# A prologue that loads x three quarters by crossbar and one quarter through TensorE

## The chip, the cores and the metric

One core of a Trainium2 chip. The metric is device microseconds (us) of one execution. A profile gives the span of one execution (about 1.8 us less than the time) and the mean clock that TensorE was granted, 1.0 being full. All runs told here were correct. The batches of runs (e1 to e4, e5 to e8, e9 to e12) carry different chip numbers in the record, so times are compared within a batch, or as ratios to the kernel before in the same rounds.

## The reference

Two branches share one input x (2048 x 640, bf16): a gated long convolution, and an attention with 32 query heads over one key/value head of width 20. A sigmoid gate mixes them.

```
g = sigmoid((x * gate_w).sum(-1))
q = x @ wq   (32 heads of 20);  k = x @ wk;  v = x @ wv
b = softmax(q k^T / sqrt(20)) v, heads joined, @ wo
a = x * (conv(kv, ssm_k) + kv * ssm_D),  kv = shift_conv(k_in) * v_in
out = g * a + (1 - g) * b
```

## The kernel before

The program is planned statically. Python code adds operations with planned costs and dependencies to a graph; a list scheduler places each on an engine at a planned time; each engine then gets its instructions in that order and waits on semaphores. An engine takes the next instruction of its list and nothing else (in the changed kernel q's first projection had its operands at 10.27 us and started at 13.34, behind a block that TensorE was still waiting for), so a wrong planned time becomes a wrong order.

```python
# Scheduler.place: the plan's model of a DMA
begin = max(start + 0.1, self.dma_bw)
self.dma_bw = begin + op.nbytes / 300e3
op.end = self.dma_bw + op.lat          # lat is 2.2 unless given
self.t[e] = start + 0.35
# pick_pe: dummy matmuls on TensorE where its planned load is low (FILL = 0.5)
if (... self.main_started and self.can_fill and m is not None and gap > 0.1
        and self.busy_in(t, 2.4) < FILL):
    f = Op("pe", self.filler, ...)
...
# loads: x transposed by the DMA crossbar, in four blocks of 512 tokens
for b in range(NB):
    o = T["xT"][:, :, 512 * b:512 * b + 512]
    i = aps["A_q"][0][512 * b:512 * b + 512, :]
    xl = self.g.add("sp", lambda e, o=o, i=i: e.dma_start_transpose(o, i), (), [("xT", b)], 0.1,
                    kind="d", nbytes=1000000, prio=-8 + b)
...
# kproj: kT groups, then k/v/gate projections per block ("kvn"), their squares, max over all blocks
gr = self.group("kT", (1.16 if b == 0 else 4.0) + 0.1 * b, banks=ALLB)
...
# qproj: needs xT block 0 and the padded wq; squares -> q2 -> "ci"; with the max of k: a row of
# bounds "cr", sent by DMA into qT ("crow"); the first scores (QK) need that row
```

So before the first score, ScalarE's first exponential can't start: k of all four blocks, its maximum, the row, its DMA. After that the kernel is 970 exponentials of 128x1024 on ScalarE, with everything else placed around them.

Of the kernel before, what the change touches and what calls it, by code (L numbers as in the profile page):

```python
# [21 lines left out]
class Op:  # L22
    __slots__ = ("eng", "fn", "deps", "cost", "kind", "name", "prio", "grp", "alts", "port", "nbytes", "main",
                 "cont", "nun", "succ", "ready", "start", "end", "placed", "sig", "value", "lane", "known", "seq",
                 "banks", "last", "floating", "tail", "attached", "lat")

    def __init__(self, eng, fn, cost, kind, name, prio):
        self.eng = eng
        self.fn = fn
        self.deps = set()  # L30
        self.cost = cost
        self.kind = kind
        self.name = name
        self.prio = prio
        self.grp = None
        self.alts = None
        self.port = False
        self.nbytes = 0
        self.main = False
        self.cont = False  # L40
        self.nun = 0
        self.succ = []
        self.ready = 0.0
        self.start = None
        self.end = None
        self.placed = False
        self.sig = False
        self.value = None
        self.lane = None
        self.known = None  # L50
        self.seq = -1
        self.banks = None
        self.last = False
        self.floating = False
        self.tail = ()
        self.attached = False
        self.lat = 2.2


class Group:  # L60
# [74 lines left out]
class Scheduler:  # L135
# [177 lines left out]
    def place(self, op, e):  # L313
        t = self.t[e]
        op.eng = e
        if op.alts:
            for x in op.alts:
                self.cand[x].discard(op)
            op.fn, op.cost = op.alts[e]
        else:  # L320
            self.cand[e].discard(op)
        if op.main and e == "pe":
            for b in op.banks or ():
                if not self.bank_claimed[b]:
                    self.bank_claimed[b] = True
                    op.deps.update(self.bank_last[b])
        start = max(t, op.ready)
        if op.kind == "d":
            begin = max(start + 0.1, self.dma_bw)
            self.dma_bw = begin + op.nbytes / 300e3  # L330
            op.end = self.dma_bw + op.lat
            self.t[e] = start + 0.35
            best = min(range(NLANES), key=lambda l: self.lanes[l][-1].end if self.lanes[l] else -1.0)
            op.lane = best
            if self.lanes[best]:
                op.deps.add(self.lanes[best][-1])
            self.lanes[best].append(op)
            op.value = 16 * len(self.lanes[best])
        else:
            if (op.port and e == "dve") or e == "pool":  # L340
                start2 = max(start, self.port_until)
                op.end = start2 + op.cost
                self.port_until = op.end
            else:
                op.end = start + op.cost
            self.t[e] = op.end
        op.start = start
        op.placed = True
        if e == "pe" and op.cost > 0.05:
            self.active.append((op.end - op.cost * 0.92, op.end))  # L350
        if op.name == "pv":
            self.can_fill = not op.last
        self.order[e].append(op)
        self.linear.append(op)
        gr = op.grp
        if gr is not None:
            if e == "pe" and op in gr.mms:
                gr.pos += 1
                if gr.pos == len(gr.mms):
                    self.open = None  # L360
            elif op in gr.evacs:
                if all(x.placed for x in gr.evacs):
                    b = gr.bank
                    self.bank_busy[b] = False
                    self.bank_last[b] = [gr.mms[-1]] + list(gr.evacs)
                    self.bank_ready[b] = max(x.end for x in gr.evacs) + LAT
        for s in op.succ:
            s.nun -= 1
            lat = 0.0 if (s.eng == "pe" and e == "pe") else LAT
            s.ready = max(s.ready, op.end + lat)  # L370
            sg = s.grp
            if sg is not None and s.eng == "pe" and not (op.grp is sg):
                sg.nun -= 1
                sg.ready = max(sg.ready, op.end + lat)
                if sg.nun == 0:
                    self.gcand.add(sg)
            if s.nun == 0:
                self.enable(s)
# [72 lines left out]
NSC, NDC, NB = 16, 5, 4  # L451
# [37 lines left out]
class Kernel:  # L489
# [163 lines left out]
    def loads(self):  # L653
        T, aps = self.T, self.aps
        x = aps["A_q"][0].rearrange("(i p) d -> p i d", p=128)
        self.dma(T["wkv"][:, :, 0:20], aps["B_wk"].rearrange("(dc p) c -> p dc c", p=128), writes=["wk"],
                 nbytes=50000, eng="act", prio=-98.8)
        self.dma(T["wkv"][:, :, 20:40], aps["B_wv"].rearrange("(dc p) c -> p dc c", p=128), writes=["wv"],
                 nbytes=50000, eng="act", prio=-98.7)
        wq = aps["B_wq"].rearrange("(dc p) n -> p dc n", p=128)  # L660
        self.dma(T["gw5"][:, :], aps["gate_w"].rearrange("(dc p) -> dc p", p=128), writes=["gw5"], nbytes=2000,
                 eng="act", prio=-98.5)
        self.dma(T["wqst"][:, :, 0:160], wq[:, :, 0:160], writes=[("wqst", 0)], nbytes=204800, eng="act", prio=-98.9)
        xl = None
        for b in range(NB):
            o = T["xT"][:, :, 512 * b:512 * b + 512]
            i = aps["A_q"][0][512 * b:512 * b + 512, :]
            xl = self.g.add("sp", lambda e, o=o, i=i: e.dma_start_transpose(o, i), (), [("xT", b)], 0.1, kind="d",
                            nbytes=1000000, prio=-8 + b)

        self.xl = [xl]
        self.dma(T["wqst"][:, :, 160:640], wq[:, :, 160:640], writes=[("wqst", 1)], nbytes=614400, prio=-4,
                 after=self.xl)
        self.dma(T["Dbc"][:, :], aps["A_ssm_D"].partition_broadcast(128), writes=["Dbc"], nbytes=163840, prio=30,
                 after=self.xl)

    def consts(self):
# [16 lines left out]
        P(lambda e: e.memset(T["vaug"][:, :, 20:21], 1.0), (), ["vaug"], 0.3, prio=-8)  # L694
        identv = T["ident"][:, :].rearrange("p (r c) -> p r c", c=32)
        V(lambda e: e.tensor_reduce(T["acol"][:, :], identv[:, :, 0:20], AX.X, ALU.add), ["ident"], ["acol"], 0.3,
          prio=-4)
        V(lambda e: e.tensor_reduce(T["mcol"][:, :], identv[:, :, 20], AX.X, ALU.add), ["ident"], ["mcol"], 0.2,
          prio=-5)
        V(lambda e: e.tensor_scalar(T["mcol"][:, :], T["mcol"][:, :], -1.0, None, ALU.mult), ["mcol"], ["mcol"], 0.2,  # L700
          prio=-5)
        V(lambda e: e.tensor_reduce(T["altcol"][:, :], T["ident"][:, 1:128:2], AX.X, ALU.add), ["ident"], ["altcol"],
          0.3, prio=-3)
        V(lambda e: e.tensor_scalar(T["altcol"][:, :], T["altcol"][:, :], -2.0, 1.0, ALU.mult, ALU.add), ["altcol"],
          ["altcol"], 0.2, prio=-3)
        for n, ng in (("IndG2", 2), ("IndG4", 4)):
            P(lambda e, n=n: e.memset(T[n][:, :, :], 0.0), (), [n], 0.2, prio=-7)
            for gl in range(ng):
                V(lambda e, n=n, gl=gl, ng=ng: e.tensor_copy(T[n][:, gl, gl:4 * ng:ng], T["acol"][:, :]), ["acol"],
                  [n], 0.2, prio=-2 if ng == 2 else 20)  # L710

        V(lambda e: e.memset(T["scl0"][:, :], 2.0 / L), (), ["scl0"], 0.1, prio=12)
        V(lambda e: e.memset(T["scl0"][0:1, :], 1.0 / L), (), ["scl0"], 0.1, prio=12)
# [77 lines left out]
    def weights2(self):  # L791
# [5 lines left out]
        for q in range(1, 4):  # L797
            self.pool(lambda e, q=q: e.tensor_copy(dst[:, :, 8 * q:8 * q + 8, 0:20], src[:, :, 8 * q:8 * q + 8, :]),
                      [("wqst", 1)], [("wq_pad", 1)], 1.5, prio=-4, name="wq_cp")

    def load_x(self):
        T = self.T
        x = self.aps["A_q"][0].rearrange("(i p) d -> p i d", p=128)
        for b in range(NB):
            self.dma(T["xn"][:, 4 * b:4 * b + 4, :], x[:, 4 * b:4 * b + 4, :], writes=[("xn", b)], nbytes=655360,
                     prio=30 + b, name="ld_x", after=self.crow0)

    def kproj(self):
# [3 lines left out]
        gr = self.group("gwt", 0.0, banks=ALLB)  # L812
        self.mm(gr, lambda e, bk: e.transpose(self.bank_bf(bk, NDC), T["gw5"][:, :], T["ident"][0:NDC, 0:NDC]),
                ["gw5", "ident"], 0.1)
        self.evac(gr, "dve", lambda e, bk: e.tensor_copy(T["wkv"][:, :, 40], self.bank_bf(bk, NDC)), (), ["wg"], 0.2)
        for b in range(NB):
            gr = self.group("kT", (1.16 if b == 0 else 4.0) + 0.1 * b, banks=ALLB)
            self.kTg.append(gr)
            for dc in range(NDC):
                self.mm(gr, lambda e, bk, b=b, dc=dc: e.matmul(  # L820
# [47 lines left out]
    def qproj(self, I, gs, prio, banks, ng):  # L868
# [22 lines left out]
        for gl in range(ng):  # L891
# [9 lines left out]
        self.dve(lambda e: e.tensor_scalar(cr[0:n, :], ci[0:n, :].bitcast(F32), T["kmaxr"][0:n, 0:1], -UP,  # L901
                                           ALU.mult, ALU.add), ["ci", "kmaxr"], ["cr"], c_fast(512), prio=pr, name="root")
        o = self.dma(qt[20:128:32, gs[0]:gs[0] + ng, :], cr[0:n, :], reads=["cr"],
                 writes=[("qT", par, gi) for gi in gs], nbytes=n * 1024, prio=pr, name="crow")
        if I == 0 and gs[0] == 0:
            self.crow0 = [o]

# [443 lines left out]
    def build(self):  # L1351
# [2 lines left out]
        self.consts()  # L1354
        self.tables()
        self.weights()
        self.kproj()
        ALLB = (7, 5, 4, 3, 2, 1, 0)
        for b in range(4):
# [81 lines left out]
```

## Time and profile before

| part of the profiled execution | us |
|---|---|
| up to the first exponential | 24.3 |
| stream of exponentials, first start to last end | 893.5 |
| of which ScalarE waits (stream less its busy time) | 2.9 |
| tail | 9.2 |
| span | 927.0 |
| time, median of the three runs at hand | 928.67 (927.61 to 930.36) |

The three parts add up to the span, so a change of the prologue is read from the first line. The prediction shows the lines of the profile.

### The profile page before, as it was taken

To read this page: it belongs to the slowest core of one execution; us is meant where nothing else is said; L and a number is where in the kernel's file an instruction comes from. 1 tells how busy PE (TensorE), PEld (TensorE's weight loads), DVE (VectorE), ACT (ScalarE), POOL (GpSimd) and SP (SyncE) were. 2 spreads that over 40 slices of the span, in tenths; PEclk is the share of its full clock that TensorE was granted. 3 is DMA by queue.
4 is the path that set the end of the run, shared out by engine and by line. 5 is a ranking of instruction groups with operands and counts; after the bars stand their busy time and mean duration, and the time that the engine had idled before them with its cause. 6 is when DMAs were issued, how large, how long until landed. Compare 5 with 4: busy or idle time off the path is not lost.

```text
span 927.0 us, 16240 instructions
## 1 busy us (share of the span) xinstructions
PE 802.8 (87%) x6829; PEld 332.5 (36%) x6829; DVE 607.5 (66%) x810; ACT 901.0 (97%) x989; POOL 377.9 (41%) x331
## 2 busy tenths in 40 slices
PE   8777788889999889999898899988999889888786
PEld 3222113433344334444343344443444433332232
DVE  6667883566675665676776677567667665567564
ACT  4999999999999999999999999999999999999996
POOL 2960001768714227733267333488433882000000
PEclk9999989999999999999999999999999997999999
DMA  7822532001000001000001020000000003111100
GB/s 159 288 74 89 195 121 65 13 9 39 19 19 19 19 8 35 19 19 19 18 14 30 19 54 18 19 13 8 18 19 18 13 13 82 38 55 49 34 13 28
DMA packets 42998, 41.83 MB, mean 45 GB/s; under 512 B 22739, under 2 KB 36173, under 8 KB 42925
## 3 DMA queue, kind: packets, MB, share of 16 engines
q1 hardware_dynamic: 40659, 40.22, 14.3%
q8 instruction: 53, 0.87, 0.4%
q10 hardware_dynamic: 2266, 0.59, 0.3%
q14 instruction: 20, 0.16, 0.1%
HBM read 31.76 MB, written 6.02 MB: 41 GB/s over the span
## 4 chain that ended last, share of the span: by engine, by line
ACT 93%; PE 5%; DVE 0%; issue 0%; DVEq 0%; POOL 0%; POOLq 0%
ACT ET L950 93%; PE ps L1386 1%; PE ps L934 1%; PE ps L1382 1%; PE ps L976 1%; PE ps L820 0%; PE ps L1232 0%; PE ps L1094 0%; PE ps L876 0%; PE ps L1296 0%; PE ps L1178 0%; DVE outsb L1116 0%; PE ps L1101 0%; PE ps L834 0%; DVEq L445 0%
## 5 line engine op out<-in xcount | busy, mean ns | idle before, releaser
L950 ACT ACTIVATE ET<-ps 128x1024 bf16<-128x1024 f32 x970 | 890.6, 1198 | 5.7 <-PE ps L934 5.1
L934 PE MATMUL ps<-qT,kT 21*128 21x512 bf16 x2048 | 225.0, 389 | 107.3 <-ACT ET L950 101.0
L1263 POOL TENSOR_TENSOR Pp<-X,K 128x512 f32<-128x512 bf16 x120 | 163.3, 1387 | 286.7 <-DVE K L1251 286.7
L976 PE MATMUL ps<-ET,vaug 128*32 128x512 bf16 x1940 | 208.8, 394 | 1.0 <-ACT ET L950 1.0
L934 PEld LDWEIGHTS ps<-qT,kT 21*128 21x128 bf16 x2048 | 56.4, 91 | 275.3 <-ACT ET L950 267.3
L964 DVE TENSOR_SCALAR dJ<-ps 128x1024 uint32<-128x1024 f32 x54 | 66.1, 1224 | 46.8 <-PE ps L934 46.4
L976 PEld LDWEIGHTS ps<-ET,vaug 128*32 128x32 bf16 x1940 | 52.3, 93 | 118.1 <-issue 113.7
L1263 POOL TENSOR_TENSOR AB<-Pp 128x256 bf16<-128x256 f32 x80 | 81.2, 1014 | 6.1
L1296 PE MATMUL ps<-AB,Tcos 128*128 128x256 bf16 x320 | 76.8, 276 | 1.3 <-DVE K L1251 1.2
L972 DVE SCALAR_TENSOR_TENSOR ETd<-dJ,dE 128x1024 bf16<-128x1024 f32 x54 | 76.4, 1415 | 0.9
L969 DVE SCALAR_TENSOR_TENSOR dE<-dJ,dE 128x1024 f32<-128x1024 uint16 x54 | 75.5, 1399 | 0.6
L971 DVE SCALAR_TENSOR_TENSOR dJ<-dJ 128x1024 f32<-128x1024 uint16 x54 | 71.2, 1318 | 0.6
L1296 PE MATMUL ps<-AB,Tsin 128*128 128x256 bf16 x280 | 67.6, 274 | 0.0
L1382 PE MATMUL ps<-Tcos,zeros 128*128 128x512 bf16 x207 | 67.0, 403 | 0.0
L1263 POOL TENSOR_TENSOR Pp<-Pp 128x512 f32<-128x512 f32 x40 | 58.8, 1469 | 3.1
L1243 DVE TENSOR_SCALAR X<-ps 128x512 bf16<-128x512 f32 x35 | 24.1, 688 | 50.1 <-PE ps L1232 49.8
L1232 PE MATMUL ps<-ssm_kT,Tsin 128*128 128x256 bf16 x320 | 50.4, 274 | 0.0
L1034 DVE COPY acc<-ps 128x512 f32<-128x512 f32 x31 | 21.4, 691 | 41.5 <-PE ps L976 41.0
L1232 PE MATMUL ps<-kv,Tcos 128*128 128x256 bf16 x320 | 47.1, 276 | 1.6 <-DVE K L1251 1.2
L1232 PE MATMUL ps<-kv,Tsin 128*128 128x256 bf16 x320 | 48.2, 274 | 0.0
L967 DVE TENSOR_SCALAR dE<-dJ 128x1024 uint32<-128x1024 uint32 x54 | 45.6, 845 | 1.4
L876 PE MATMUL ps<-xT,wq_pad 128*128 128x512 bf16 x160 | 44.0, 382 | 1.9 <-DVE qT L544 1.1
(133 smaller groups left out, 733.9 us busy)
## 6 DMA issues: line engine op xcount, KB each, us to landing
kslab<-in_A_k_dram SPq DMA_DIRECT2D x15, 640.0 KB
rbc<-scr_d SPq DMA_DIRECT2D x31, 256.0 KB
scr_o<-oTn SPq DMA_DIRECT2D x24, 128.0 KB
vslab<-in_A_v_dram SPq DMA_DIRECT2D x16, 160.0 KB, 3.2
xn<-in_A_q_dram SPq DMA_DIRECT2D x4, 640.0 KB
kst<-in_A_ssm_k_dram SPq DMA_DIRECT2D x5, 512.0 KB
out_dram<-outsb SPq DMA_DIRECT2D x14, 160.0 KB
oTp<-scr_o SPq DMA_DIRECT2D x12, 160.0 KB, 2.9
```

Of the source, the lines that this page charges most:

```text
L934: o = op("pe", lambda e, r=r, Iu=Iu, g=g, j=j, bk=banks[r]: e.matmul(self.bank(bk), T["kT4"][32 * r:32 * r + 21, 128 * j:128 * j + 128], T ...
L950: op("act", lambda e, p=p, slot=slot: e.activation(T[f"ET{slot}"][:, :], self.ps[:, 1024 * p:1024 * p + 1024], ACT.Exp, scale=SCALE), [("p ...
L964: V(lambda e, p=p: e.tensor_scalar(J[:, :], self.ps[:, 1024 * p:1024 * p + 1024], SCALE * LOG2E * 65536.0, EOFF * 65536.0, ALU.mult, ALU.add),
L967: V(lambda e: e.tensor_scalar(E[:, :], J[:, :], 7, 0x7F800000, ALU.logical_shift_left, ALU.bitwise_and), [kJ], ["dE"], c_fast(1024), **k)
L969: V(lambda e: e.scalar_tensor_tensor(Ef, lo, ED, Ef, ALU.add, ALU.mult), [kJ, "dE"], ["dE"], c_ps(1024), **k)
L971: V(lambda e: e.scalar_tensor_tensor(Jf, lo, EP, lo, ALU.add, ALU.mult), [kJ], [kJ], c_ps(1024), **k)
L972: V(lambda e: e.scalar_tensor_tensor(T["ETd"][:, :], Jf, EQ, Ef, ALU.add, ALU.mult), [kJ, "dE"], ["ETd"], c_ps(1024), **k)
L976: return op("pe", lambda e, r=r, j=j, src=src: e.matmul(self.bank(6)[32 * r:32 * r + 32, :], T["vaug"][:, j, :], src[:, 512 * (r % 2):512 ...
L1232: o = self.mm(gr, lambda e, bk, lhs=lhs, rhs=rhs, comp=comp, n=n: e.matmul(self.bank(bk, 256, 256 * comp), lhs, rhs, start=(n == 0), stop= ...
L1263: f = lambda e: e.tensor_tensor(out, a, b, alu)
L1296: self.mm(gr, lambda e, bk, lhs=lhs, fc=fc, comp=comp, h=h: e.matmul(self.bank(bk, 256, 256 * h), lhs, AB[:, fc, :, comp, :], start=(fc == ...
L1382: sch.filler = lambda e: e.matmul(self.bank(6), self.T["zeros"][:, :], self.T["Tcos"][:, 0, 0:512], start=False, stop=False)
```

## The change

Its intent: a crossbar transpose keeps the SyncE queue for 3.3 us (13.20 us for the four in the kernel before), so one of the four is replaced by a plain row load and transposes on an idle TensorE; small constants come earlier, kT groups leave the banks of the first scores alone, and the plan gets new figures for DMAs. Core of the diff:

```diff
-                 eng="act", prio=-98.5)                       # gate_w
-        self.dma(T["wqst"][:, :, 0:160], ..., eng="act", prio=-98.9)
+                 eng="act", prio=-98.65)
+        self.dma(T["wqst"][:, :, 0:160], ..., eng="act", prio=-98.6)
+        self.dma(T["xn"][:, 12:16, :], x[:, 12:16, :], writes=[("xn", 3)], nbytes=655360, prio=-9)
-        for b in range(NB):
+        for b in range(NB - 1):
             ... dma_start_transpose ...
-                            nbytes=1000000, prio=-8 + b)
+                            nbytes=655360, prio=-8 + b, lat=1.6)
+            xl.iss = 3.3
@@ Scheduler.place
-            op.end = self.dma_bw + op.lat
-            self.t[e] = start + 0.35
+            op.end = max(self.dma_bw, start + op.iss) + op.lat
+            self.t[e] = start + op.iss
@@ consts: acol, mcol and IndG2 to prio -1996..-1994, altcol to 5; gate column's copy to -2000
+    def xT(self):          # block 3: 20 transposes on TensorE in three groups, copied to xT by VectorE or ScalarE
+        ...
@@ kproj
-            gr = self.group("kT", ..., banks=ALLB)
+            gr = self.group("kT", ..., banks=ALLB if b == 0 else (7, 4, 5))
@@ qproj: the row of bounds is planned with lat=1.7 in place of 2.2
@@ load_x: three blocks of rows instead of four
```

More of the change, by code (lines that the diff above doesn't have):

```diff
@@ L24 @@
                  "cont", "nun", "succ", "ready", "start", "end", "placed", "sig", "value", "lane", "known", "seq",
-                 "banks", "last", "floating", "tail", "attached", "lat")
+                 "banks", "last", "floating", "tail", "attached", "lat", "iss")
     def __init__(self, eng, fn, cost, kind, name, prio):
@@ L57, in __init__ @@
         self.lat = 2.2
+        self.iss = 0.35
 class Group:
@@ L661, in loads @@
         self.dma(T["gw5"][:, :], aps["gate_w"].rearrange("(dc p) -> dc p", p=128), writes=["gw5"], nbytes=2000,
-                 eng="act", prio=-98.5)
-        self.dma(T["wqst"][:, :, 0:160], wq[:, :, 0:160], writes=[("wqst", 0)], nbytes=204800, eng="act", prio=-98.9)
+                 eng="act", prio=-98.65)
+        self.dma(T["wqst"][:, :, 0:160], wq[:, :, 0:160], writes=[("wqst", 0)], nbytes=204800, eng="act", prio=-98.6)
         xl = None
-        for b in range(NB):
+        x = aps["A_q"][0].rearrange("(i p) d -> p i d", p=128)
+        self.dma(T["xn"][:, 12:16, :], x[:, 12:16, :], writes=[("xn", 3)], nbytes=655360, prio=-9)
+        for b in range(NB - 1):
             o = T["xT"][:, :, 512 * b:512 * b + 512]
@@ L696, in consts @@
         V(lambda e: e.tensor_reduce(T["acol"][:, :], identv[:, :, 0:20], AX.X, ALU.add), ["ident"], ["acol"], 0.3,
-          prio=-4)
+          prio=-1996)
         V(lambda e: e.tensor_reduce(T["mcol"][:, :], identv[:, :, 20], AX.X, ALU.add), ["ident"], ["mcol"], 0.2,
-          prio=-5)
+          prio=-1995)
         V(lambda e: e.tensor_scalar(T["mcol"][:, :], T["mcol"][:, :], -1.0, None, ALU.mult), ["mcol"], ["mcol"], 0.2,
-          prio=-5)
+          prio=-1995)
         V(lambda e: e.tensor_reduce(T["altcol"][:, :], T["ident"][:, 1:128:2], AX.X, ALU.add), ["ident"], ["altcol"],
-          0.3, prio=-3)
+          0.3, prio=5)
         V(lambda e: e.tensor_scalar(T["altcol"][:, :], T["altcol"][:, :], -2.0, 1.0, ALU.mult, ALU.add), ["altcol"],
-          ["altcol"], 0.2, prio=-3)
+          ["altcol"], 0.2, prio=5)
         for n, ng in (("IndG2", 2), ("IndG4", 4)):
-            P(lambda e, n=n: e.memset(T[n][:, :, :], 0.0), (), [n], 0.2, prio=-7)
+            P(lambda e, n=n: e.memset(T[n][:, :, :], 0.0), (), [n], 0.2, prio=-9.7)
             for gl in range(ng):
                 V(lambda e, n=n, gl=gl, ng=ng: e.tensor_copy(T[n][:, gl, gl:4 * ng:ng], T["acol"][:, :]), ["acol"],
-                  [n], 0.2, prio=-2 if ng == 2 else 20)
+                  [n], 0.2, prio=-1994 if ng == 2 else 20)
         V(lambda e: e.memset(T["scl0"][:, :], 2.0 / L), (), ["scl0"], 0.1, prio=12)
@@ L799, in weights2 @@
                       [("wqst", 1)], [("wq_pad", 1)], 1.5, prio=-4, name="wq_cp")
+    def xT(self):
+        T = self.T
+        b = NB - 1
+        for d0, nd in ((0, 2), (2, 2), (4, 1)):
+            gr = self.group("xT", 1.0, banks=(0, 1, 2, 3, 4, 5, 7))
+            for dc in range(d0, d0 + nd):
+                for ci in range(4):
+                    i = 4 * b + ci
+                    self.mm(gr, lambda e, bk, i=i, dc=dc, ci=ci, d0=d0: e.transpose(
+                        self.bank_bf(bk, 128, 512 * (dc - d0) + 128 * ci), T["xn"][:, i, 128 * dc:128 * dc + 128],
+                        T["ident"][:, :]), [("xn", b), "ident"], 0.09)
+            out = T["xT"][:, d0:d0 + nd, 512 * b:512 * b + 512]
+            al = self.copy_alts(out, lambda bk, nd=nd: self.bank_bf(bk, 512 * nd).rearrange(
+                "p (d t) -> p d t", d=nd), True)
+            self.evac(gr, "dve", None, (), [("xT", b)], 0.45, alts=al)
     def load_x(self):
@@ L803, in load_x @@
         x = self.aps["A_q"][0].rearrange("(i p) d -> p i d", p=128)
-        for b in range(NB):
+        for b in range(NB - 1):
             self.dma(T["xn"][:, 4 * b:4 * b + 4, :], x[:, 4 * b:4 * b + 4, :], writes=[("xn", b)], nbytes=655360,
@@ L814, in kproj @@
                 ["gw5", "ident"], 0.1)
-        self.evac(gr, "dve", lambda e, bk: e.tensor_copy(T["wkv"][:, :, 40], self.bank_bf(bk, NDC)), (), ["wg"], 0.2)
+        self.evac(gr, "dve", lambda e, bk: e.tensor_copy(T["wkv"][:, :, 40], self.bank_bf(bk, NDC)), (), ["wg"], 0.2,
+                  prio=-2000.0)
         for b in range(NB):
-            gr = self.group("kT", (1.16 if b == 0 else 4.0) + 0.1 * b, banks=ALLB)
+            gr = self.group("kT", (1.16 if b == 0 else 4.0) + 0.1 * b, banks=ALLB if b == 0 else (7, 4, 5))
             self.kTg.append(gr)
@@ L903, in qproj @@
         o = self.dma(qt[20:128:32, gs[0]:gs[0] + ng, :], cr[0:n, :], reads=["cr"],
-                 writes=[("qT", par, gi) for gi in gs], nbytes=n * 1024, prio=pr, name="crow")
+                 writes=[("qT", par, gi) for gi in gs], nbytes=n * 1024, prio=pr, name="crow", lat=1.7)
         if I == 0 and gs[0] == 0:
@@ L1356, in build @@
         self.weights()
+        self.xT()
         self.kproj()
```

## The prediction

> **What bounds the kernel now.** I read the page first (busy shares, chain), then the chain in order of time for the first 30 us, then the order of instructions there, then the waits of the SyncE queue, and last the DMA rate in half-microsecond windows.
>
> From the page, the shares of the chain and the costliest group:
>
> ```profile
> ACT 93%; PE 5%; DVE 0%; issue 0%; DVEq 0%; POOL 0%; POOLq 0%
> ...
> L950 ACT ACTIVATE ET<-ps 128x1024 bf16<-128x1024 f32 x970 | 890.6, 1198 | 5.7 <-PE ps L934 5.1
> ```
>
> The span of 927.0 us is one stream of 970 exponentials on ScalarE. They keep it busy for 890.6 us and it waits 5.7 us in all, of which 2.8 us is the wait for the first score. So there are three parts: 24.3 us before the first exponential, about 893.5 us of stream, 9 us of tail. The change touches only the first. Whatever it wins there comes out one for one as long as the stream itself doesn't change; its ceiling is a fraction of 24.3 us, 2.6% of the time.
>
> The chain in the first 30 us, in order of time (start, length, what):
>
> ```profile
> 12.97 1.29 PE ps L1386 x6
> 14.26 0.58 PE ps L892 x2
> 14.87 0.68 DVE ci L898
> 15.55 0.10 DVE wkv L815
> 15.64 0.05 issue
> 15.69 0.89 PE ps L834 x29
> ...
> 18.15 1.30 PE ps L1386 x6
> 19.45 0.18 PE ps L853
> 19.64 3.34 PE ps L820 x15
> 22.98 0.89 issue
> 23.87 0.45 PE ps L934 x4
> 24.33 6.51 ACT ET L950 x7
> ```
>
> L1386 are dummy matmuls[...], so the names hide the causes. Those are seen in the order of instructions:
>
> ```profile
> 0.73 13.20 SPq L668 DMA_TRANSPOSE xT<-in_A_q_dram  x4
> 13.81 0.85 DVE L709 CAST IndG<-acol 128x4 bf16<-128x4 f32 x6
> 14.23 0.09 PEld L892 LDWEIGHTS ps<-sq,IndG 128*8 128x8 bf16 x2 [0.47 <-DVE IndG L709]
> 15.48 0.16 DVE L815 COPY wkv<-ps 128x5 bf16<-128x5 bf16 x1
> 18.62 0.24 ACT L840 ACTIVATE ksq<-ps 128x80 f32<-128x80 f32 x1 [0.45 <-PE ps L834]
> 20.84 0.73 SPq L511 DMA_DIRECT2D qT<-cr  x1
> 23.02 0.75 DVE L825 TENSOR_SCALAR kT<-ps,mcol 128x512 bf16<-128x512 f32 x1 [0.33 <-PE ps L820]
> ```
>
> Three knots: (a) VectorE makes the small indicator tile only at 13.8 us; TensorE, in order, waits for it, and the gate column (L815) and the k/v projections (L834) follow only from 15.69. (b) The fourth crossbar transpose is issued until 13.93, and the SyncE queue is released by its landing at 16.07 (2.1 us of wait below). The projection of block 3 starts at 17.48, so this was close behind the knot (a) rather than the first bound. (c) The row of bounds goes out at 20.84 and lands before 22.70; the first scores still start only at 23.87, because the eviction of the last kT group (23.02 + 0.75 = 23.77) held a bank they write.
>
> ```profile
> SPq L511 <- DMA xT<-in_A_q_dram: 2.1, 1, 2.1
> ```
>
> Do the transposes wait for the DMA engines or for the queue that issues them? Half-microsecond windows (window, length, busy of PE, PEld, DVE, ACT, POOL, clock, DMA share, GB/s) around the third and fourth:
>
> ```profile
> 11.00:11.50 0.50, 0.50 (x4) 0.20 (x2) 0.50 (x2) 0.37 (x1) 0.00 (x0) 1.00 1.28 291
> ...
> 13.00:13.50 0.50, 0.50 (x4) 0.24 (x3) 0.42 (x1) 0.50 (x1) 0.00 (x0) 1.00 0.48 33
> 13.50:14.00 0.50, 0.50 (x4) 0.15 (x2) 0.50 (x4) 0.42 (x2) 0.00 (x0) 1.00 1.16 258
> ```
>
> In bursts they move 291 GB/s and fall to 33 between: 655 KB take about 2.25 us of each 3.3 us. The issue is the limit, the engines have about 1 us spare in each period.
>
> [...]here issuing time is what counts: 13.20 / 4 = 3.30 us for each transpose against 0.4 to 0.7 us for a plain load in this trace. [...]291 in the burst and 655 KB / 3.30 us = 199 GB/s over the period. [...]the trace has such transposes later (L1178: 219 ns, issued about 95 ns apart by the weight loads) and their copies (L1181, 128x1024 bf16 from PSUM: 0.69 us). [...]
>
> **The change part by part.**
>
> 1. *One transpose less on the queue, one row load before.* Minus 3.30 us, plus about 0.5 us of issue. Three transposes are issued from 0.73 + 0.5 = 1.2 to 11.1 us; with 2.1 us to land, the last block is there at 13.25 instead of 16.05. The load's 655 KB come in front, when the ScalarE loads (256 KB) also run. In the kernel before, 2.0 to 6.0 us moved some 260 GB/s. Load, weights and first transpose (1,566 KB) would need 1,566 / 265 = 5.9 us, until about 7.9; the second transpose then flows to 10.2 and the third (issued 7.8 to 11.1) to 12.6 to 12.9. So the spare microsecond of each period absorbs most of the load; I allow 0 to 0.7 us. Landing: 13.3 to 14.
>
> 2. *Transposing the fourth block on TensorE.* 20 transposes x about 0.1 us = 2 us of TensorE, in time it spent on dummies (18 of them before 8.4 us). Copies: two of 1024 columns x 0.69 + one of 512, about 0.4 = 1.8 us on VectorE or ScalarE. Off the chain unless VectorE is full: it was busy for 12.0 of the first 15.7 us.
>
> 3. *Early small constants and gate column.* The indicator tile (0.23 for acol, 0.3 for mcol, two casts) comes right after the tables, about 10 us, and the gate column when its tiny load has landed. Knot (a) vanishes; 3.5 us of the 15.69 are freed, and the landing of the last block takes over as bound. altcol and four casts (0.9 us) move behind, which pays half of the copies.
>
> 4. *Small weights.* In this diff they were on the ScalarE queue already; only the order changes: wk, wv, gate first, wq's first part last, issued near 2.5 instead of 0.74. It lands perhaps at 6 to 7 instead of before 3.8; its copy takes 1.1 us, so q's first projection starts at 8 to 8.5, as it did (8.27). No gain.
>
> 5. *From the last block to the first exponential.* From the trace: the block's first projection matmul to its square 0.88 us (15.69 to 16.57 for block 0); from the square to the row's landing 22.70 - 18.62 = 4.08; to the scores 0.1; scores to exponential 0.45. Sum 5.5 us. But the three kT groups of 3.34 us run in front of the scores, from 1.02 us after the square: 0.88 + 1.02 + 3.34 + 0.06 + 0.45 = 5.75 us, the later of the two. In the kernel before this stretch took 17.48 to 24.32 = 6.84, of which the bank's eviction was 0.8 to 0.9: kT groups limited to banks 7, 4, 5 leave the banks of the first scores free and save it.
>
> Sum: 13.3 + 5.75 = 19.05 in the best case; with 0 to 0.7 us for the load and about 0.3 us for VectorE or TensorE being late, 19.7. First exponential at 24.3 - 4.6 = 19.7, so 928.7 - 4.6 = 924.1 us.
>
> 6. *Later.* The fourth xn load leaves the 26 to 32 us stretch (655 KB less where the DMA is full). ScalarE is saturated there: nothing. The schedule of the filler work shifts; the stream's other waits sum to 5.7 - 2.8 = 2.9 us, so perhaps 1 us either way.
>
> **The rivals.** *VectorE becomes the bound.* Work up to the maximum of k was about 13.9 us of busy time by 19.2 (summed from my two-microsecond windows); minus 0.9 deferred, plus up to 1.8 of copies, makes 14.8 us, and only 12.5 us pass between 0.8 and 13.3. For it: the sum, and that squares of q rank low and ScalarE is full with sine tables. Against it: ScalarE may take copies, and the last block's own evictions come after 13.3. If so the row leaves 1 to 1.5 us later: first exponential 20.8, time 925.3. *The row load pushes the transposes one for one*[...]: 1.9 to 2.3 us given back, first exponential near 21.5, time 925.9. Against it stand the gaps of 33 GB/s. *The fourth transpose was hidden anyway*, and only the knots (a) and (c) pay: then the constants alone would move the projections until block 3's landing at 16.05, which gives 21.8 and 926.2; this needs the row path to be no earlier than the crossbar, which I doubt. *The gain is taken back in the stream* by a new wait for kT or q groups: these are due several exponentials (1.2 us records, 0.92 us apart) after the start, and nothing in the profile shows ScalarE waiting there; 926 to 928.
>
> **Range and chances.** Centre 924.1; 922.0 if the landing and all else go as in the best case and the stream wins a little; 926.4 if two of the rivals act together. A 2% change would be 18.6 us, which is three quarters of the whole prologue: faster has 0.5%. Slower by 2% would need a stream stall of 18 us[...]: 1%. Within 2%: 98.5%.
>
> **What would show it.** Right: the SyncE queue shows three transposes over some 9.9 us after one plain load; the last projection group (L834 before) starts at 13.3 to 14.3; the scores start without a bank eviction just before them; the first exponential at 19 to 20.5; the stream from there about 893.5 us long. Wrong: transposes slower than 3.3 us or landing after 14.5 (load contends); VectorE without gaps from 1 to 15 us and the square waiting for it (VectorE bound); or a first exponential near 19.7 with no shorter time (stream stalls).

The landing at 13.3 and the 5.75 us after it make 19.05, with the allowances 19.7, and so 924.1 us. From the trace of the kernel before: 3.30 us for the issue of a transpose, 291 GB/s in the burst and 199 over the period, and, for 128x128 transposes on TensorE ("such transposes"), 219 ns each, about 95 ns apart, with copies of 0.69 us. The 260 GB/s of part 1 are what the trace shows from 2.5 to 5.5 us (231 to 277 in half-microsecond windows); from 2.0 to 6.0 it is 229.

## The result, and the profile after

The changed kernel took 929.78 us (median of 6 runs, 928.89 to 932.90) against 929.04 for the kernel before (6 runs). The ratio is 1.0013 with a 95% interval of 0.9995 to 1.0031. So: no gain, where I had put 924.1 and a range up to 926.4.

The chain's shares and the costliest group, from the page of the changed kernel:

```profile
ACT 93%; PE 5%; DMA 1%; SPq 1%; DVE 0%; DVEq 0%; issue 0%
...
L972 ACT ACTIVATE ET<-ps 128x1024 bf16<-128x1024 f32 x970 | 890.3, 1213 | 2.4 <-PE ps L956 2.0
```

The stream is the same work (890.3 us busy, before 890.6). New are a DMA and the SyncE queue on the chain. Its first 25 us in order of time (start, length, what):

```profile
1.25 4.93 SPq L671
...
6.23 6.41 DMA xT<-in_A_q_dram
...
12.69 0.82 PE ps L856 x20
13.51 3.59 PE ps L898 x10
17.10 1.08 PE ps L842 x5
...
18.98 1.28 ACT L747
...
21.52 3.34 PE ps L842 x15
...
25.07 0.40 PE ps L956 x4
25.48 1.93 ACT ET L972 x2
```

The first exponential starts at 25.46, 1.1 us later than before. The first crossbar issue took 4.93 us, and TensorE's k/v projections of a block (L856) wait for a landing at 12.64. Only after them do q's projections (L898) run, 3.59 us for ten matmuls that took 2.16 before. The order of TensorE and of the SyncE queue in that stretch:

```profile
0.74 0.46 SPq L512 DMA_DIRECT2D xn<-in_A_q_dram  x1
1.25 11.81 SPq L671 DMA_TRANSPOSE xT<-in_A_q_dram  x3
9.82 0.66 PE L856 MATMUL ps<-wkv,xT 128*128 128x41 bf16 x20 [0.83 <-DMA xT<-in_A_q_dram]
12.69 0.82 PE L856 MATMUL ps<-wkv,xT 128*128 128x41 bf16 x20 [1.98 <-DMA xT<-in_A_q_dram]
13.34 3.76 PE L898 MATMUL ps<-xT,wq_pad 128*128 128x512 bf16 x10
15.18 0.39 SPq L512 DMA_DIRECT2D wqst<-in_B_wq_dram  x1
```

Blocks 0 and 1 are used as they land, near 9.8 and 12.6; the plan had them 3.4 us earlier. The wqst load waits for the last crossbar block, which therefore landed at 15.18, not at 13.3 to 14. q's projection needed only block 0 and a weight copy (on GpSimd) that ended at 10.27, but it stands in the list behind block 1. So of its 5 us of delay (13.34 where 8.3 was expected) 2 us are operands that came late, and 3 us the order. And q's projection then ran at half clock, seen in these windows (start and end, length, busy of PE, PEld, DVE, ACT, POOL, granted clock, DMA share, GB/s):

```profile
10.70:12.70 2.00, 0.02 (x2) 0.02 (x2) 0.24 (x1) 0.59 (x2) 0.00 (x0) 1.00 0.85 133
12.70:16.10 3.40, 3.40 (x27) 1.67 (x28) 2.13 (x10) 0.66 (x2) 0.00 (x0) 0.52 0.66 144
16.10:17.10 1.00, 1.00 (x5) 0.39 (x4) 0.00 (x0) 1.00 (x3) 0.00 (x0) 0.91 0.54 75
```

After 2.0 us with TensorE idle (and 0.88 us busy in the 1.4 us before, 9.30 to 10.70), the next 3.4 us run at a granted clock of 0.52, which is just when q's projection comes. That the pause brought the half clock on is not shown: in e7 TensorE waited 1.6 us for the same block, and its clock stayed at 1.00 from 9 to 19 us. Executions of one kernel differ: in the 29 runs of the kernel before that the experiments list with their clocks, the time falls by 0.44 us for each 0.001 of mean clock (fit over clocks of 0.985 to 0.996, correlation -0.78). That is a correlation and not yet a cause.

### The profile page after: what moved, and what is told of

Read it like the earlier page. It is cut to its first block, busy times and chain, and to the rows that moved or that the text cites. A ratio compares the mean times of both kernels' runs of the same rounds, so it can differ in the third digit from the quotient of the medians.

```text
span 928.0 us, 16257 instructions
## 1 busy us (share of the span) xinstructions
PE 804.4 (87%) x6836; PEld 333.9 (36%) x6836; DVE 615.4 (66%) x808; ACT 903.9 (97%) x994; POOL 390.3 (42%) x331
## 4 chain that ended last, share of the span: by engine, by line
ACT 93%; PE 5%; DMA 1%; SPq 1%; DVE 0%; DVEq 0%; issue 0%
ACT ET L972 93%; PE ps L956 1%; PE ps L1405 1%; PE ps L998 1%; DMA xT<-in_A_q_dram 1%; SPq L671 1%; PE ps L842 0%; PE ps L1318 0%; PE ps L898 0%; PE ps L1116 0%; PE ps L1123 0%; PE ps L1254 0%; DVE outsb L1138 0%; ACT L747 0%; PE ps L856 0%; DVEq L446 0%
## 5 line engine op out<-in xcount | busy, mean ns | idle before, releaser
L972 ACT ACTIVATE ET<-ps 128x1024 bf16<-128x1024 f32 x970 | 890.3, 1213 | 2.4 <-PE ps L956 2.0
L1285 POOL TENSOR_TENSOR Pp<-X,K 128x512 f32<-128x512 bf16 x120 | 170.3, 1446 | 276.7 <-DVE K L1273 276.7
L1285 POOL TENSOR_TENSOR AB<-Pp 128x256 bf16<-128x256 f32 x80 | 84.4, 1055 | 5.9
L991 DVE SCALAR_TENSOR_TENSOR dE<-dJ,dE 128x1024 f32<-128x1024 uint16 x54 | 79.4, 1471 | 0.4
L993 DVE SCALAR_TENSOR_TENSOR dJ<-dJ 128x1024 f32<-128x1024 uint16 x54 | 75.1, 1391 | 0.8
L1405 PE MATMUL ps<-Tcos,zeros 128*128 128x512 bf16 x213 | 70.8, 409 | 0.0
L1285 POOL TENSOR_TENSOR Pp<-Pp 128x512 f32<-128x512 f32 x40 | 61.3, 1532 | 3.1
L898 PE MATMUL ps<-xT,wq_pad 128*128 128x512 bf16 x160 | 44.9, 393 | 1.4 <-DVE qT L545 1.0
```

The lines of the kernel that those rows point to most:

```text
L972: op("act", lambda e, p=p, slot=slot: e.activation(T[f"ET{slot}"][:, :], self.ps[:, 1024 * p:1024 * p + 1024], ACT.Exp, scale=SCALE), [("p ...
L991: V(lambda e: e.scalar_tensor_tensor(Ef, lo, ED, Ef, ALU.add, ALU.mult), [kJ, "dE"], ["dE"], c_ps(1024), **k)
L993: V(lambda e: e.scalar_tensor_tensor(Jf, lo, EP, lo, ALU.add, ALU.mult), [kJ], [kJ], c_ps(1024), **k)
L1285: f = lambda e: e.tensor_tensor(out, a, b, alu)
L1405: sch.filler = lambda e: e.matmul(self.bank(6), self.T["zeros"][:, :], self.T["Tcos"][:, 0, 0:512], start=False, stop=False)
```

## The experiments

Time up to the first exponential ("first"), landing of the last crossbar block, and the stream are read from the profiled execution of each kernel; "waits" is the stream less ScalarE's busy time in it. All outputs are right. The batches of runs are e1 to e4, e5 to e8, e9 to e12.

| kernel | last block landed | first | stream | waits | clock | median time (runs) | ratio to before (95%) |
|---|---|---|---|---|---|---|---|
| before | 16.07 | 24.3 | 893.5 | 2.9 | 0.987 | 929.04 (6) | |
| changed | 15.18 | 25.5 | 891.8 | 1.4 | 0.983 | 929.78 (6) | 1.0013 (0.9995 to 1.0031) |
| e1 true landings in the plan | 14.93 | 22.0 | 896.1 | 5.5 | 0.987 | 928.88 (4) | 1.0002 (0.9988 to 1.0017) |
| e2 four crossbar blocks | 15.85 | 22.6 | 897.6 | 6.7 | 0.984 | 929.89 (4) | 1.0005 (0.9975 to 1.0036) |
| e3 row load on ScalarE's queue | 14.35 | 22.8 | 896.0 | 5.3 | 0.988 | 932.94 (4) | 1.0038 (1.0016 to 1.0060) |
| e4 before + bank limit | 15.97 | 23.3 | 892.9 | 2.5 | 0.992 | 929.59 (4) | 1.0007 (0.9985 to 1.0029) |
| e5 before, start held back | 16.06 | 25.7 | 892.9 | 2.7 | 0.991 | 930.26 (6) | 1.0018 (0.9995 to 1.0041) |
| e6 before, filled to 0.8 | 15.83 | 25.5 | 891.5 | 1.4 | 0.998 | 928.14 (6) | 0.9985 (0.9966 to 1.0004) |
| e7 changed, filled to 0.8 | 15.29 | 24.0 | 897.4 | 6.6 | 0.990 | 932.72 (6) | 1.0035 (1.0013 to 1.0057) |
| e8 = e1 filled to 0.8 | 14.81 | 22.0 | 891.8 | 1.6 | 0.998 | 924.58 (6) | 0.9952 (0.9933 to 0.9971) |
| e9 row load last | 12.54 | 24.8 | 896.6 | 6.0 | 0.984 | one look | |
| e10 = e2 filled to 0.8 | 17.68 | 25.6 | 892.5 | 2.2 | 0.994 | 925.06 (6) | 0.9959 (0.9933 to 0.9985) |
| e11 changed, filled to 0.95 | 14.90 | 23.7 | 898.4 | 2.5 | 0.997 | 933.32 (6) | 1.0046 (1.0024 to 1.0068) |
| e12 = e1 filled to 0.95 | 15.23 | 22.0 | 898.0 | 2.5 | 0.997 | 930.71 (6) | 1.0010 (0.9991 to 1.0029) |

Four groups of the same prologue can be read from it. The prologue of the kernel before (unaltered in e6; in e5 less the 1.2 us hold) starts the stream at 24.3, 24.5 and 25.5; that of the changed kernel (e7, e11) at 25.5, 24.0 and 23.7; that of e2 (e10) at 22.6 and 25.6; that of e1 (e8, e12) at 22.0 three times. So one profile can be 1 to 3 us off another of the same prologue, and a difference of that size between two kernels needs more than their two profiles. In the kernel before the spread has a visible cause: TensorE starts with 18 dummies, which follow each other at 0.43 us until the trace's first record of full clock and then at 0.22 us. In the profile of the kernel before this record comes at 5.9 us, after 7 of them; in that of e6 at 8.1 us, after 12 (first the kernel before, then e6):

```profile
2.96 5.47 PE ps L1386 x18
...
3.22 6.45 PE ps L1386 x18
```

**e1, the order.** Theory: the landings are given, but the order planned from wrong landings costs most of the gain.

```diff
-                            nbytes=655360, prio=-8 + b, lat=1.6)
-            xl.iss = 3.3
+                            nbytes=655360, prio=-8 + b, lat=(3.6, 3.0, 2.1)[b])
+            xl.iss = (5.0, 3.4, 3.4)[b]
```

> The changed kernel with one thing altered: the static scheduler is told when the three crossbar blocks really landed in the changed kernel's trace (about 9.7, 12.6 and 15.1 us) in place of some 3.4 us earlier. The data moved and their queue stay the same; only the order of instructions changes (q's first projection goes ahead of the k/v projection of block 1). Theory 'order': TensorE no longer stands 2 us at block 1 with its clock falling to half, q's projection takes 2.2 us instead of 3.6, ScalarE's exp table is in by 16.5 instead of 20.3; first exponential at 22.5 to 23.5 instead of 25.5, time about 2 to 3 us less than the changed kernel. Rival 'landing': only the landing of the last block counts, the order costs nothing; first exponential stays at 25 to 25.5 and the time stays.

Measured: first exponential at 22.01, half a microsecond better than the range given, with the last block at 14.93, nearly as late as in the changed kernel. TensorE in order:

```profile
10.08 0.66 PE L856 MATMUL ps<-wkv,xT 128*128 128x41 bf16 x20
10.80 2.10 PE L898 MATMUL ps<-xT,wq_pad 128*128 128x512 bf16 x9
12.74 1.24 PE L842 MATMUL ps<-xT,wk 128*128 128x512 bf16 x5
13.82 1.89 PE L856 MATMUL ps<-wkv,xT 128*128 128x41 bf16 x60
```

q's projection now runs at 10.8 at full clock, before block 1. So the order cost 3.45 us of prologue against the changed kernel's profile; 1.44 of that was the half clock (25.46 against 24.02 in e7, the same prologue without the half clock). In e7 q's projection waits as long but then runs at full clock, 2.16 us for its ten matmuls in place of 3.59:

```profile
13.40 2.16 PE ps L898 x10
```

Against the other two profiles of the changed prologue, e1 starts 2.0 and 1.7 us earlier. But the second half of the expectation failed: the time stayed at that of the kernel before, because the stream grew to 896.1 us with 5.5 us of waits.

**e2, four crossbar blocks with the rest of the change.** The row load, the `xT` method and its call are taken out, the loops go over four blocks again, and the plan's `lat` for them is 2.0.

> The changed kernel with its first part undone: all four x blocks by crossbar, no row load ahead of them, no TensorE transposes; the reordered small loads, early constants and gate column, the bank limit and the shorter planned latency stay. If the prediction's own chain (last landing + 5.75 us) holds, the fourth block lands at 16.05 as in the kernel before and the first exponential starts at 21.8 to 22.5, so the rest of the change alone is worth 2 us and the time is near 927. Rival: the small parts are worth nothing without the crossbar part, first exponential at 24.3 as before, time as before.

Measured: first exponential at 22.59, landing 15.85. In this profile the early constants, the bank limit and the plan's new figures alone bring 1.7 us of prologue, close to the 2 expected, and the crossbar part adds only 0.6 us more once its order is right (e1). But the same prologue in e10 had its last block 1.8 us later and started the stream at 25.6, so these two sizes are not shown. The time didn't show a gain, again with a longer stream (897.6).

**e3, another queue for the row load.** `eng="act", prio=-98.5` in place of `prio=-9`.

> The changed kernel with the row load issued by the ScalarE queue after the small weights instead of by SyncE in front of the transposes. Theory 'queue': the row load in front holds up the issue of the first transpose (4.9 us in place of 3.3); off that queue all three issues take 3.3 us, the SyncE queue is released at 12.7 to 13.3 instead of 15.2, first exponential 22 to 23.5. Rival 'engines': the 16 DMA engines are what is short, so the same bytes from another queue delay the transposes as much: release at 14.5 to 15.2.

Measured: release at 14.35, below the range of the rival "engines" (14.5 to 15.2), but nearer to it than to the theory's. One transpose took 5.58 us to issue here too, though no row load stood ahead of it on its queue. So the load held up the transposes from either queue (the third landed at 15.18 and at 14.35, against 12.54 in e9). The time was 0.4% longer than before, with waits of 5.3 us and a lower mean clock in the other three runs (0.980 to 0.984).

**e4, the bank limit alone.** In the kernel before, `banks=ALLB if b == 0 else (7, 4, 5)`.

> The kernel before with one part of the change: kT groups 1 to 3 may use banks 7, 4, 5 only. Theory: the first scores no longer wait for the eviction of the last kT group (23.77); they start when kT's matmuls end at 23.0, first exponential at 23.4 instead of 24.3, time 0.9 less (near the noise). Rival: the row of bounds lands later than it seems and the scores stay at 23.9.

Measured: 23.27 in place of 24.32, as expected for the prologue. The pause of 0.89 us between the last kT matmuls and the first scores, which the prediction shows for the kernel before, is gone; only 0.1 us of the difference is an earlier start of q's projection (8.34 against 8.43):

```profile
19.70 3.19 PE L820 MATMUL ps<-xT,wk 128*128 128x512 bf16 x14 [0.16 <-issue]
22.82 0.39 PE L934 MATMUL ps<-qT,kT 21*128 21x512 bf16 x4
```

Nothing shows in the time (1.0007, interval of 0.4%).

**e5, is the stream elastic?** e1 and e2 raised the question whether an earlier start is worth anything. In the kernel before, ScalarE is held back just ahead of the first exponential:

```diff
+                    if e == "act" and op.name == "exp" and first:
+                        first = False
+                        for _ in range(12):        # 1-element Exp into a scratch tile
+                            self.hold(eng, _)
```

> The kernel before with the same orders on every engine and twelve one-element exponentials (about 0.2 us each) put on ScalarE just ahead of the first large one: first exponential at about 26.7 instead of 24.3. Theory 'the stream is rigid': a start later by 2.4 us makes the kernel 2.4 us slower, so a start that much earlier should be worth as much. Rival 'the stream is elastic' (something else sets its end, so that starts within a few us don't matter, which would explain why the early start of e1 was worth nothing): time within 0.7 us of the kernel before.

Measured: the hold was 1.2 us and not 2.4, since the small instructions overlapped (twelve in 1.23 us, where a single one-element activation shows 0.20). The stream kept its length (892.9), the time rose by 0.18% = 1.7 us, with an interval of -0.05 to 0.41%. This fits a rigid stream and doesn't exclude the rival. Inconclusive.

**e6, e7, e8: filling the stream.** Theory "clock": ScalarE's waits in the stream are episodes of half TensorE clock. In all profiles without added filling nearly all waits (90% or more) lie in such episodes or in the 2 us after them; for e1, these windows (columns as above):

```profile
776.00:780.00 4.00, 2.16 (x22) 0.61 (x19) 1.05 (x2) 4.00 (x6) 2.87 (x4) 1.00 0.00 0
780.00:784.00 4.00, 4.00 (x21) 1.21 (x20) 3.93 (x5) 2.84 (x4) 0.00 (x0) 0.53 0.66 173
784.00:788.00 4.00, 4.00 (x25) 2.01 (x24) 1.34 (x2) 2.63 (x3) 0.00 (x0) 0.62 0.50 149
```

TensorE is 54% busy from 776 to 780, then has a granted clock of 0.53 and 0.62 for two windows, and ScalarE, which was busy all the time, loses 1.2 and 1.4 us. The edit makes the plan put a dummy matmul wherever TensorE's planned load over 2.4 us is below 0.8:

```diff
-                    and self.busy_in(t, 2.4) < FILL):      # the filler of the stream; FILL = 0.5
+                    and self.busy_in(t, 2.4) < 0.8):
```

> The kernel before with dummy matmuls added in the stream whenever the planned load of TensorE over 2.4 us is below 0.8 instead of 0.5. Theory 'clock': ScalarE's waits in the stream come from episodes of half TensorE clock after thin stretches; with the stretches filled these mostly vanish (mean clock over 0.995 against 0.987), waits in the stream fall from 2.9 us to about 1, time 1 to 2 us less than before. Rival 'fillers get in the way': more matmuls delay scores, ScalarE waits more, time up by several us.

> The changed kernel with the same added dummy matmuls in the stream. Theory 'clock': with the stream made steady, the time differs from that of the kernel before with the same filling (e6) by the difference of the first exponentials, about +1.1 us. Rival: no relation, the difference is anything from -2 to +3.

> e1 (the changed kernel planned with the true landings, first exponential at 22.0) with the same added dummy matmuls in the stream. Theory 'clock': the 5.5 us of waits in its stream shrink to about 1 and the early start shows: 2.3 us less than e6 and 3 to 4 us less than e7, about 925. Rival: as e1, 929.

Measured: e6 went as expected in its profile (clock 0.998, waits 1.4), time 0.9985, not clear of noise. e8 went as expected: waits 1.6 in place of 5.5, stream 891.8, time 924.58, 0.48% below the kernel before and clear of noise. Against e6, in the same rounds, that is 3.6 us less, with a start 2.3 to 3.5 us earlier. The same stretch in e8:

```profile
776.00:780.00 4.00, 2.90 (x29) 0.95 (x26) 2.62 (x4) 4.00 (x6) 0.12 (x1) 0.97 0.25 70
780.00:784.00 4.00, 4.00 (x26) 2.00 (x24) 3.71 (x4) 3.07 (x4) 0.00 (x0) 0.61 0.59 154
784.00:788.00 4.00, 4.00 (x41) 1.83 (x37) 0.71 (x2) 3.66 (x4) 0.00 (x0) 1.00 0.76 178
```

One episode remains there and ends a window earlier. e7 missed badly: expected 1.1 us above e6, measured 4.6 above. Its waits are again half-clock episodes (5.9 of 6.6 us, near 118, 786 and 871), which the filling did not remove. In front of the last one:

```profile
865.11 0.40 PE L998 MATMUL ps<-ET,vaug 128*32 128x512 bf16 x4
866.62 0.40 PE L956 MATMUL ps<-qT,kT 21*128 21x512 bf16 x4 [1.11 <-ACT ET L972]
```

TensorE pauses for 1.1 us where a group of heads ends, and there the plan's rule allows no dummy (`can_fill` is false after the last product of a group). I didn't test whether that gap starts the episode.

**e9, the row load last.** `prio=-5.5` in place of -9, so that it follows the three transposes.

> The changed kernel with the row load issued behind the three transposes on the same queue instead of ahead of them. If the load's bytes are what delays the transposes (engines), they are now undisturbed: issues of 3.3 us each, the third landed at 12.7, 3.3 earlier than the fourth of the kernel before and 2.5 earlier than in the changed kernel; the row load then lands near 14.5 to 15 and is the last to come. If the transposes are slow for another reason (the reordered small loads), the third still lands after 14. First exponential at 24 to 25.5: the TensorE transposes and their copies now come last.

```profile
0.73 9.72 SPq L671 DMA_TRANSPOSE xT<-in_A_q_dram  x3
10.50 0.59 SPq L512 DMA_DIRECT2D xn<-in_A_q_dram  x1
12.54 0.38 SPq L512 DMA_DIRECT2D wqst<-in_B_wq_dram  x1
```

Measured: undisturbed, the three transposes are issued in 9.72 us (3.24 each) and landed by 12.54; in the changed kernel 11.81 and 15.18. So the row load in front costs 2.6 us of the 3.3 us that the missing transpose saves. The reordered small loads, the same in both, are not the cause. One issue took 3.16 to 3.33 us in the kernel before and 2.69 to 3.66 in e2; beside a row load one of the three took 4.85 to 5.59 (the changed kernel, e1, e3, e7, e8). As expected the row load then came last (14.82) and the start was at 24.8.

**e10, e11, e12.** e10 is e2 with the filling of 0.8; e11 and e12 are e7 and e8 with 0.95.

> e2 (all four blocks by crossbar, the rest of the change kept) with the stream filled to 0.8 as in e6 to e8. Tells what the crossbar part itself is worth once the order is right: first exponential 22.6 against 22.0 of e8, so if first exponentials decide in a filled stream, time 0.6 us above e8: 925.2. Rival: four transposes cost 2 us or more, 927.

> The changed kernel with the stream filled to 0.95 instead of 0.8. e7 kept three half-clock episodes and 6.6 us of waits in spite of the filling. Theory 'clock': if the stronger filling removes them (mean clock over 0.996), waits drop under 2 us and the time is 926 to 927.5, close to e6. Rival: it is the order of the stream itself that makes ScalarE wait, time stays at 931 to 933 whatever the clock.

> e8 with the filling at 0.95. Theory 'clock': clock near 1.0 already, nothing left to win, 924 to 925. Rival 'fillers get in the way' at this density: 926 or more.

Measured: e10's median is 925.06, as expected and not to be told from e8 (different rounds, intervals overlap widely), though its profiled execution was a poor one: the last transpose landed at 17.7, TensorE's clock fell to half from 18 to 22 (0.77, 0.50, 0.50 and 0.52 by the microsecond), and the stream started at 25.6. Its six times spread from 922.91 (clock 1.000) to 929.01 (0.994). e11 and e12 both missed the theory; in e12 the rival "fillers get in the way" came true. Their clock is steady (0.997) and the waits are 2.5 us, but the stream grows to 898 us: exponentials occupy ScalarE for 895.8 and 895.5 us in place of some 890. A single one did not get longer: its mean length on the page is 1070 ns in e11 against 1177 in e8. They overlap less, so that each starts later after the one before: 920 to 925 ns in 323 of 969 cases (169 in e8), where most follow after 904. So at this density the fillers get in the way, through short delays that the count of waits doesn't show; what causes these is open. With a clock equally steady, the two kernels differ by 2.6 us, and their first exponentials by 1.7.

## Why the prediction was wrong

- *What bounds the kernel.* Right: a prologue, a stream, a tail; 970 exponentials of 890 us in every kernel but e11 and e12.
- *Part 1, the landing.* Wrong in size. I allowed "0 to 0.7 us" for the row load and put the landing at 13.3 to 14. It was 15.18; without the load in front 12.54 (e9), so the term is 2.6 us. I had argued from windows of 33 GB/s between bursts that the spare microsecond would absorb it. The first issue grew from 3.2 to 4.9 us instead. My second rival ("one for one", 1.9 to 2.3 us given back) had this right.
- *Part 4, "q's first projection starts at 8 to 8.5".* This is the step that failed most. It started at 13.34. Two things were wrong. The operands came later than I had them: block 0 at 9.8, where my sum has the first transpose done at 7.9, and the weights at 9.4 instead of 6 to 7, which makes 10.27 with the copy. And I let each engine take up its work when its operands come, but the order is fixed by the plan, and the plan had the blocks 3.4 us early; this cost the other 3 us. My chain from the true landing would give 15.18 + 5.75 = 20.9; the profile has 25.46. e1 changes nothing but planned times and gets 3.45 us of these 4.5 back, 1.44 of them a half clock that I had not thought of. The other microsecond remains in e1: there ScalarE is busy until 16.4 with sine tables and the exp table load before it takes the last squares, and it evicts the last kT group (0.69 us) right before the first exponential.
- *Part 5, banks.* Right: 0.8 to 0.9 us saved were expected; in e4 the pause of 0.89 us is gone.
- *Rival "VectorE becomes the bound".* Wrong: VectorE waited 5.5 us for squares in the changed prologue, three times.
- *"Comes out one for one as long as the stream itself doesn't change".* The condition failed. I gave the stream's waits "perhaps 1 us either way"; among kernels without added filling they ranged from 1.4 to 6.7 us. e1 won 2.3 us in the prologue and its stream was 2.6 us longer. This is also what became of my rival "the gain is taken back in the stream", though not by the wait for kT or q groups that I had named. With the stream filled (e8 against e6) the early start shows in the time. That nearly all waits come with half-clock episodes is shown by every profile without added filling; that thin stretches of TensorE start them is argued from the windows and from e6 and e8, and e7 shows that filling to 0.8 is no sure remedy. Nor does the length of the episodes decide: by the clock records of the traces the kernel before, the changed kernel and e1 each had 23.9 us of half clock in their streams, and waited 2.9, 1.4 and 5.5 us. So something else decides, perhaps where an episode falls; that isn't tested.

For the changed kernel itself the account is: its prologue starts the stream at 23.7 to 25.5 us over three profiles, the old one at 24.3 to 25.5, so there was hardly a gain to lose; in the compared profiles the start was 1.1 us later, the stream 1.7 us shorter and the tail 1.6 us longer, the last with a granted clock of 0.82 (0.50 from 918 to 920) where the tail before had 1.00. Open are why the changed order's stream suffers more from the clock under filling (e7 against e6), and how much of the spread between executions (5.7 us over those 29 runs) comes from where the stretches of half clock fall.

e8 beats both kernels: 924.58 us, where the kernel before took 929.72 in the same rounds. Not shown is that the fourth block through TensorE has a part in this: e10, with four crossbar blocks, has a ratio of 0.9959, and e8 of 0.9952.

## What to carry to other kernels

In a statically ordered program the planned landing of a DMA is as important as the real one: a landing planned too early puts work that is ready behind work that isn't. Here blocks planned 3.4 us early cost 3.45 us of the prologue, 1.44 of them in a stretch at a granted clock of 0.52 that followed 2.0 us of idle TensorE in one of the profiles. When you put a load in front of other transfers, count its bytes against theirs even where the queue's issue time seems to be the limit (2.6 us here, with 33 GB/s between the bursts). And before crediting a start that comes earlier, split the span into prologue, stream and tail, and check that the rest stayed equally long; here the stream moved by more than the gain.
